# Two heads per softmax step in an attention and expert kernel: 64-row score tiles, and division after the product with v

## The chip, the cores and the metric

The kernel runs on one core of a Trainium2 chip. The metric is the time of one execution on the device in microseconds. Three runs of the kernel before took 1354.6, 1354.81 and 1356.63 us; the median is 1354.81 us.

The core has a matrix engine (TensorE, PE in the profile; its weight loads are shown as PEld), a vector engine (VectorE, DVE), an activation engine (ScalarE, ACT), a general engine (GpSimd, POOL) and a queue that issues transfers (SyncE, SP). Each runs its own instructions in order and they meet at semaphores. The matrix engine writes to PSUM, a small memory of eight banks, from which DVE and ACT read.

## The reference

Attention with a threshold over 8 batches of 8 heads, 576 positions and 64 values per head, and behind it a two-layer network on all 4608 tokens:

```python
scale = 1.0 / np.sqrt(q.shape[-1])
scores = scale * np.matmul(q, k.transpose(0, 1, 3, 2))
thresh = np.max(scores, axis=-1, keepdims=True) - tau
scores = np.where(scores >= thresh, scores, -1000000000.0)
scores = scores - np.max(scores, axis=-1, keepdims=True)
attn = np.exp(scores)
attn = attn / (np.sum(attn, axis=-1, keepdims=True) + 1e-09)
attn_out = np.matmul(attn, v)                      # (8, 8, 576, 64)

x = attn_out.transpose(0, 2, 1, 3).reshape(8 * 576, 512)
h = x @ w_in                                       # 512 -> 2048
g = h * (1.0 / (1.0 + np.exp(-h)))
return g @ w_out                                   # 2048 -> 512
```

## The kernel before

**Precision.** Products run in pieces. q and k are split into a rounded part and the rest (`hi`, `lo`); so are the attention weights, v, x, the weights of the network and its inner values, in 16 bits. A product is the sum of the partial products of the pieces.

**Visits and tiles.** Attention goes through *visits* of two heads, a pair. Batch 0 is visited twice, first for queries 0 to 255 (`low`) and then for the rest (`high`); from batch 1 on there is one visit (`all`) per pair, 28 in all. A visit consists of tiles of 128 queries of one head against all 576 keys. The last 64 queries of both heads share a tile, so a full visit has nine tiles. There are 288 tiles: 16 low, 20 high and 252 in batches 1 to 7. The low tiles work in float32 throughout (`direct`) and are transposed on PE.

**A tile's way.** 
- `scores` (line 406): the 64 rows of q's `hi` stand above the 64 of its `lo` (`qstack`), k's rows stand there twice, so that a matmul over 128 rows gives both partial products. Four matmuls of 288 columns per tile, eight for the shared one. The result lies in a PSUM buffer of two banks; there are two such buffers (`ps_s`).
- `soft1` (416, 419): DVE takes the negated maximum, then the threshold. `soft1b` (426): ACT takes the exponential. `soft2` (435, 439, 443): DVE sets what is under the threshold to zero and sums the rest, then adds 1e-9 and takes the reciprocal. The score buffer is free after line 435.
- `soft2b` (448): ACT multiplies the tile by the reciprocal of its row's sum, in place. `soft3` (457, 459, 462, 465): the weights are rounded to 16 bits (by POOL, for the first tiles by ACT) and POOL subtracts for the rest. `hl` holds both; SP transposes it into `wT` by a transfer (475). The float32 tile `w` has four buffers, `hl` three, `wT` three.

**Before and behind it.** `load_qk` fetches q and k of one head, each twice for the two halves of the rows. `split_k` and `split_q` (309, 310, 318, 320) make the pieces per head. `split_v` (270, 271) rounds v. `av` (490) multiplies the transposed weights with v, the two heads in the two column halves of the array, 28 matmuls per range of queries; `av_post` (508, 509) makes the two pieces of x. The experts work on ranges of queries in units: `h_unit` (524 to 547) and `o_unit` (562 to 573), twelve matmuls each, 16 + 16 units per range, two ranges of 288 queries per batch.

**Once per batch** `vscale` takes a common scale of v: a maximum per partition on DVE, then `partition_all_reduce` on POOL (line 113), then small operations on DVE (from 116 on).

**The order.** The program is written out in slots, one per tile. In each slot stand the steps of a tile, the loads and splits due, and a number of units of the experts at a rate that is set when a range becomes ready (`rate`: units waiting over the slots until the next range that is more than one slot away). A planner then orders the instructions of each engine by priority and by a modelled time; some steps are given a higher priority (`PRI_S` 500 for scores, 50 and 200 for the parts of the softmax). The weights of the network are decoded and split in slots up to 26 (`W_PLAN`).

```python
for h, use, tl, last in ((ha, u, ta, last_a), (ha + 1, use_b, tb + [4] * (4 in ta), last_b)):
    at(use - LOAD, lambda v=v, h=h: load_qk(v, h))
    at(use - 3, lambda h=h: split_k(h))
    at(use - 2, lambda h=h, tl=sorted(tl): split_q(h, tl))
for j, (c0, n) in enumerate(ranges):
    avs.setdefault(last_b + AV_LAG + j, []).append((v, p, c0, n))
```

## Time and profile before

| | |
|---|---|
| median of three runs | 1354.81 us |
| span of the profiled execution | 1360.4 us (5.6 us above the median, which is 0.4%) |
| granted TensorE clock, mean | 0.950 |
| busy: PE, DVE, ACT, POOL | 1183.7, 1002.8, 817.5, 789.9 us |
| read from HBM, written | 66.72 MB, 9.44 MB |
| DMA packets | 363479, most of them under 512 B |
| transfers issued by SP | 304 transposes, 128 + 128 of q and k, 32 of v, 56 of the output |

The profiled execution's own time is its span; nothing around it is shown. An operation's row in the list of groups gives the line, the engine, the operation, what it writes and reads with shape, the count, the busy time, the mean of one in ns, and the idle time of the engine before it with what ended it. Busy time is that in which at least one instruction of the group was at work, so overlapping instructions count once. In the rows by time the first number is the start, the second the duration. In the rows of stretches, each engine's busy time stands with its count of instructions; the clock, the share of the transfer engines and GB/s end the row.

### The profile page before, as it was taken

To read this page: it belongs to the slowest core of one execution; us is meant where nothing else is said; L and a number is where in the kernel's file an instruction comes from. 1 tells how busy PE (TensorE), PEld (TensorE's weight loads), DVE (VectorE), ACT (ScalarE), POOL (GpSimd) and SP (SyncE) were. 2 spreads that over 40 slices of the span, in tenths; PEclk is the share of its full clock that TensorE was granted. 3 is DMA by queue.
4 is the path that set the end of the run, shared out by engine and by line. 5 is a ranking of instruction groups with operands and counts; after the bars stand their busy time and mean duration, and the time that the engine had idled before them with its cause. 6 is when DMAs were issued, how large, how long until landed. Compare 5 with 4: busy or idle time off the path is not lost.

```text
span 1360.4 us, 26858 instructions
## 1 busy us (share of the span) xinstructions
PE 1183.7 (87%) x9392; PEld 899.9 (66%) x9392; DVE 1002.8 (74%) x2619; ACT 817.5 (60%) x1493; POOL 789.9 (58%) x964
## 2 busy tenths in 40 slices
PE   3774787898599979898899969899799999999998
PEld 2453555666477757676677757677577777777777
DVE  4987997897598967968497856869478787872421
ACT  3776775675476756656375745757367666662432
POOL 2647984787478656754476646556467666661000
PEclk9887888999799999999899979999799999999999
DMA  6454955778467656664475556565466565543000
GB/s 226 140 185 125 197 129 94 146 139 170 88 133 155 122 106 129 131 128 86 99 132 124 118 96 136 101 127 121 82 122 116 115 129 115 106 88 53 6 19 18
DMA packets 363479, 158.15 MB, mean 116 GB/s; under 512 B 329552, under 2 KB 338256, under 8 KB 363344
## 3 DMA queue, kind: packets, MB, share of 16 engines
q1 hardware_dynamic: 363344, 156.43, 55.5%
q8 instruction: 74, 1.21, 0.4%
q14 instruction: 61, 0.50, 0.1%
HBM read 66.72 MB, written 9.44 MB: 56 GB/s over the span
## 4 chain that ended last, share of the span: by engine, by line
DVE 35%; PE 34%; issue 13%; ACT 6%; POOL 6%; DMA 5%; SPq 2%; POOLq 0%; ACTq 0%; DVEq 0%
PE o L562 15%; PE h L524 8%; DVE w L435 8%; DVE sm L416 6%; DVE gbuf L547 6%; PE s L406 5%; PE a L490 5%; DVE qstack L310 3%; DVE th L533 3%; DMA vraw<-in_vL 2%; DMA wT<-hl 2%; ACT w L426 2%; POOL hl L459 2%; POOL hl L462 2%; ACT w L448 2%
## 5 line engine op out<-in xcount | busy, mean ns | idle before, releaser
L524 PE MATMUL h<-x,wst 128*128 128x288 f16 (+2 forms) x3072 | 422.3, 290 | 22.6 <-DVE th L533 19.1
L562 PE MATMUL o<-gbuf,wst 128*128 128x288 f16 (+2 forms) x3072 | 419.4, 293 | 22.4 <-DVE gbuf L547 16.1
L562 PEld LDWEIGHTS <-wst 128*128 128x128 f16 x3072 | 296.4, 100 | 117.1 <-issue 27.1
L459 POOL TENSOR_SCALAR hl<-w 128x576 f16<-128x576 f32 x264 | 187.3, 710 | 317.9 <-ACT w L448 69.1
L524 PEld LDWEIGHTS <-wst 128*128 128x128 f16 x3072 | 290.7, 99 | 119.2 <-issue 37.5
L462 POOL TENSOR_TENSOR hl<-w,hl 128x512 f16<-128x512 f32 x272 | 332.0, 1220 | 28.0 <-issue 13.9
L426 ACT ACTIVATE w<-s,sm 128x576 f32<-128x576 f32 x288 | 211.0, 736 | 204.5 <-POOL hl L465 135.4
L435 DVE SCALAR_TENSOR_TENSOR w<-s,sm,w 128x576 f32<-128x576 f32 x288 | 232.6, 810 | 110.4 <-ACT w L426 108.7
L448 ACT ACTIVATE w<-w,sm 128x576 f32<-128x576 f32 x288 | 218.2, 770 | 86.5 <-DVE sm L443 81.6
L416 DVE TENSOR_REDUCE sm<-s 128x1 f32<-128x576 f32 x288 | 215.1, 748 | 44.4 <-PE s L406 42.3
L406 PE MATMUL s<-khi,qstack 128*128 128x288 f32 x608 | 160.4, 346 | 70.0 <-DVE w L435 36.9
L547 DVE SCALAR_TENSOR_TENSOR gbuf<-th,gbuf 128x288 f16<-128x288 f32 (+2 forms) x256 | 167.3, 656 | 20.9 <-ACT gbuf L541 20.2
L406 PEld LDWEIGHTS s<-khi,qstack 128*128 128x128 f32 x608 | 98.5, 198 | 98.8 <-issue 71.4
L490 PE MATMUL a<-wT,v 128*64 128x288 f16 (+1 forms) x1680 | 142.4, 294 | 16.1 <-DMA wT<-hl 15.0
L532 ACT ACTIVATE th<-h,msc 128x288 f32<-128x288 f32 (+2 forms) x256 | 126.3, 495 | 49.5 <-DVE gbuf L547 30.0
L541 ACT ACTIVATE gbuf<-th 128x288 f16<-128x288 f32 (+2 forms) x252 | 109.9, 438 | 44.5 <-DVE th L533 43.9
L406 PE MATMUL s<-klo,qstack 128*128 128x288 f32 x608 | 134.2, 304 | 0.0
L533 DVE SCALAR_TENSOR_TENSOR th<-th,h 128x288 f32<-128x288 f32 (+2 forms) x256 | 113.2, 444 | 27.6 <-ACT th L532 25.4
L490 PEld LDWEIGHTS <-v 128*64 128x64 f16 x1680 | 91.3, 110 | 56.7 <-issue 41.9
L465 POOL TENSOR_TENSOR hl<-w,hl 128x64 f16<-128x64 f32 x272 | 115.3, 424 | 0.0
L406 PEld LDWEIGHTS s<-klo,qstack 128*128 128x128 f32 x608 | 102.2, 197 | 0.0
L320 POOL TENSOR_TENSOR klo<-kraw,khi 128x576 fp32r<-128x576 f32 x64 | 95.6, 1493 | 1.4 <-ACT khi L318 1.3
(82 smaller groups left out, 868.8 us busy)
## 6 DMA issues: line engine op xcount, KB each, us to landing
qraw<-in_qT SPq DMA_DIRECT2D x128, 144.0 KB, 3.0
kraw<-in_kT SPq DMA_DIRECT2D x128, 144.0 KB, 3.0
vraw<-in_vL SPq DMA_DIRECT2D x32, 320.0 KB, 3.5
wraw<-in_w_out SPq DMA_DIRECT2D x16, 512.0 KB, 4.0
out_t<-ot SPq DMA_DIRECT2D x56, 144.0 KB, 2.0
wT<-hl SPq DMA_TRANSPOSE x304, 3.3
gbuf<-in_w_in SPq DMA_DIRECT2D x8, 512.0 KB, 5.1
wraw<-in_w_in SPq DMA_DIRECT2D x8, 512.0 KB, 4.9
```

The lines of the kernel that those rows point to most:

```text
L406: nc.tensor.matmul(s_ps[:, j, :HALF], lhs, kk[:, j * HALF : (j + 1) * HALF], start=(n == 0), stop=(n == len(seq) - 1),)
L416: nc.vector.tensor_reduce(out=negm, in_=s_ps[:, :, :HALF], op=ALU.max, axis=AX.XY, negate=True)
L426: nc.scalar.activation(wtile[t].rearrange("p (j c) -> p j c", j=2), sps[t][:, :, :HALF], AF.Exp, bias=small[t][:, 0:1],)
L435: nc.vector.scalar_tensor_tensor(out=w3, in0=s_ps[:, :, :HALF], scalar=sm[:, 1:2], in1=w3, op0=ALU.is_ge, op1=ALU.mult, accum_out=sm[:, 2:3],)
L448: nc.scalar.activation(w, w, AF.Copy, scale=r)
L459: nc.gpsimd.tensor_scalar(out=fl[:, 0:S], in0=w, scalar1=1.0, scalar2=1.0, op0=ALU.mult, op1=ALU.mult)
L462: nc.gpsimd.tensor_tensor(out=fl[:, 640:1152], in0=w[:, 0:512], in1=fl[:, 0:512], op=ALU.subtract)
L490: nc.tensor.matmul(a_ps[odd * D : (odd + 1) * D, :n], vt[:, lo_v, odd, kv, :], wT[v, b * H + 2 * p + odd][:, kw, c0 - base : c0 - base + n ...
L524: nc.tensor.matmul(ph[:, :n], wi(c, f, lo_w), x16[b, lo_x][:, c, c0 : c0 + n], start=(k == 0), stop=(k == 11),)
L533: nc.vector.scalar_tensor_tensor(out=th[:, :n], in0=th[:, :n], scalar=1.0, in1=ph[:, :n], op0=ALU.add, op1=ALU.mult,)
L547: nc.vector.scalar_tensor_tensor(out=g[:, 1, :n], in0=th[:, :n], scalar=2.0**-14, in1=g[:, 0, :n], op0=ALU.mult, op1=ALU.subtract,)
L562: nc.tensor.matmul(ps[:, :n], wo(f, d, lo_w), g[:, lo_g, :n], start=(f == 0 and k == 0), stop=(f == NF - 1 and k == 2),)
```

## The change

The unit of work of the attention becomes a *step*: the same 128 queries of both heads of a pair. A full visit has four steps of two heads and one of the last 64 queries of both, five in place of nine.

- **q and k.** Both heads' rows are loaded once, one head in rows 0 to 63 and the other in 64 to 127, and split once per pair. q's rounding is with ACT and its rest always with DVE (before, with POOL in batch 0). The last queries are laid out by the host with zeros, so that one 128-row matmul serves both heads.
- **Scores.** Four partial products, each over 64 rows, for each head and half of the keys: 16 matmuls per step, the heads in turn in the upper and lower rows. The PSUM buffer has four banks, and there is one.
- **Softmax.** One reduction over both heads. The threshold goes to POOL. Exponential and select are still one per head. The sums of a visit are kept (`sums`).
- **Division.** The scaling of the weights goes, and with it the reciprocal per tile (the low visits keep both). `invert_sums` inverts the sums of a range, writes them to DRAM, and `load_rows` reads them back as rows spread over the partitions; `av_post` multiplies the product with v by them on DVE, rounds on ACT, and subtracts on POOL.
- **Rounding of the weights** is with ACT, over both heads; the subtraction is one POOL operation. `w` has two buffers of two heads, `hl` two of two heads. In the rows of `hl` the rest follows the rounded part at column 576 and not at 640, so blocks 5 to 8 of v's rounded part are shifted copies that two transfers make in `split_v`.
- **v** is loaded once more for its split from batch 1 on.
- **Ranges** are queries 0 to 255 and 256 to 575 in all batches. The first is handed on after a visit's second step, so the ranges of a batch become ready five slots apart. `wT` has three buffers for each range.
- **Slots.** A step of two heads takes two slots, the shared one takes one; the plan of the weights, rates and gaps stay. Scores of the next step are written after the select of this one.

```diff
+QW = S + 64
-LOAD = 5  # tiles that the loads of q and k run ahead
+LOAD = 6
+ROW_LAG, AV_LAG2 = 2, 4
+RANGES = [(0, 256), (256, 320)]
...
-    ps_s = ctx.enter_context(tc.tile_pool(name="ps_s", bufs=2, space=PSUM))
+    ps_s = ctx.enter_context(tc.tile_pool(name="ps_s", bufs=1, space=PSUM))
...
-        o = sb.tile([P, 2, 2, 5, D], F16, tag="v16", name=f"v16_{b}_{p}", bufs=4)
-        nc.scalar.activation(o[:, 0], t, AF.Copy, scale=s)
+        hi = sb.tile([P, 2, 9, D], F16, tag="vhi", name=f"vhi_{b}_{p}", bufs=2)
+        lo = sb.tile([P, 2, 5, D], F16, tag="vlo", name=f"vlo_{b}_{p}", bufs=2)
+        nc.scalar.activation(hi[:, :, 0:5, :], t, AF.Copy, scale=s)
...
+        nc.sync.dma_start(out=hi[0:D, :, 5:9, :], in_=hi[D:P, :, 0:4, :])
+        nc.sync.dma_start(out=hi[D:P, :, 5:9, :], in_=hi[0:D, :, 1:5, :])
...
-    def load_qk(v, h):
-        for r in range(2):
-            nc.sync.dma_start(out=kr[r * D : (r + 1) * D, :], in_=kT[b, hh])
-            nc.sync.dma_start(out=qr[r * D : (r + 1) * D, :], in_=qT[b, hh])
+    def load_qk(v):
+        kr = sb.tile([P, S], F32, tag="kraw", name=f"kraw_{v}", bufs=1)
+        nc.sync.dma_start(out=kr, in_=kT[b, p])
+        qr = sb.tile([P, QW], F32, tag="qraw", name=f"qraw_{v}", bufs=1)
+        nc.sync.dma_start(out=qr, in_=qT[b, p])
...
+    def split_q(v):
+        c0 = P * VISITS[visits[v][2]][0]
+        src = qkraw[v][0][:, c0:]
+        nc.scalar.activation(qh[:, c0:], src, AF.Copy, scale=gate)
+        nc.vector.scalar_tensor_tensor(
+            out=ql[:, c0:], in0=src, scalar=gate, in1=qh[:, c0:].bitcast(F32),
+            op0=ALU.mult, op1=ALU.subtract,
+        )
...
     def scores(t):
+        v, i = steps[t]
+        s_ps = ps_s.tile([P, 2, 2, 512], F32, tag="s", name=f"s_{t}")
+            seq = [(qh, kh), (qh, kl), (ql, kh), (ql, kl)]
+        w = P if i == 4 else D
+        for n, (qq, kk) in enumerate(seq):
+            for j in range(2):
+                for h in range(heads(t)):
+                    r = slice(h * w, (h + 1) * w)
+                    nc.tensor.matmul(
+                        s_ps[:, h, j, :HALF], qq[r, i * P : (i + 1) * P],
+                        kk[r, j * HALF : (j + 1) * HALF],
+                        start=(n == 0), stop=(n == len(seq) - 1),
+                    )
     def soft1(t):
+        w = sb.tile([P, 2, S], F32, tag="w32", name=f"w32_{t}", bufs=2)
         nc.vector.tensor_reduce(
+            out=sm[:, 0:nh], in_=s_ps[:, :nh, :, :HALF], op=ALU.max, axis=AX.XY, negate=True
+        )
+        nc.gpsimd.tensor_scalar(
+            out=sm[:, 2 : 2 + nh], in0=sm[:, 0:nh], scalar1=-1.0, scalar2=ntau,
+            op0=ALU.mult, op1=ALU.add,
+        )
...
+    def invert_sums(v, a, b):
+        nc.vector.tensor_scalar(
+            out=r[:, a:b], in0=sums[v][:, a:b], scalar1=1e-9, scalar2=None, op0=ALU.add
+        )
+        nc.vector.reciprocal(out=r[:, a:b], in_=r[:, a:b])
+        for h in range(2):
+            if a < 8:
+                nc.sync.dma_start(
+                    out=d[h, 64 * a : 64 * min(b, 8)].rearrange("(i p) -> p i", p=P),
+                    in_=r[:, a + h : min(b, 8) : 2],
+                )
...
+    def load_rows(v, g):
+        R = sb.tile([P, WID], F32, tag="rows", name=f"rows_{v}_{g}", bufs=2)
+        for h in range(2):
+            nc.sync.dma_start(
+                out=R[h * D : (h + 1) * D, :n], in_=d[h, c0 : c0 + n].partition_broadcast(D)
+            )
     def soft2b(t):
+        if steps[t][0] not in direct:
+            return
     def soft3(t):
+        hl = sb.tile([P, 2, 9 * P], F16, tag="hl", name=f"hl_{t}", bufs=2)
+        nc.scalar.activation(hl[:, :nh, 0:S], w[:, :nh], AF.Copy)
+        nc.gpsimd.tensor_tensor(
+            out=hl[:, :nh, S : 2 * S], in0=w[:, :nh], in1=hl[:, :nh, 0:S], op=ALU.subtract
+        )
...
     def av_post(v, p, g, a_ps):
+        x = sb.tile([P, WID], F32, tag="th", name=f"x32_{v}_{c0}", bufs=4)
+        nc.vector.tensor_tensor(
+            out=x[:, :n], in0=a_ps[:, :n], in1=rows.pop((v, g))[:, :n], op=ALU.mult
+        )
+        nc.scalar.activation(hi, x[:, :n], AF.Copy)
+        nc.gpsimd.tensor_tensor(out=lo, in0=x[:, :n], in1=hi, op=ALU.subtract)
...
+            if v not in direct:
+                at(u, lambda v=v, a=a, e=e: invert_sums(v, a, e))
+                at(u + ROW_LAG, lambda v=v, g=g: load_rows(v, g))
+                lag = AV_LAG2
+            avs.setdefault(u + lag, []).append((v, p, g))
             if p == NPAIR - 1:
+                ready.append((u + lag + 1, b, *RANGES[g]))
```

More of the change, by code (lines that the diff above doesn't have):

```diff
@@ L340, in scale_direct @@
+    direct = set()
     def scale_direct(v):
-        for j in range(2):
-            own = direct[v][0][j * D : (j + 1) * D, 256 * j : 256 * (j + 1)]
-            nc.scalar.activation(own, own, AF.Copy, scale=gate[j * D : (j + 1) * D, :])
+        own = qkraw[v][0][:, 0 : RANGES[0][1]]
+        nc.scalar.activation(own, own, AF.Copy, scale=gate)
     def soft3_direct(t):
         w = wtile.pop(t)
-        v, parts = tiles[t]
-        base, n = VISITS[visits[v][2]][2][0]
-        main = bank([P, 4, P], f"tm_{t}")
@@ new lines, in soft3_direct @@
+        n = RANGES[0][1]
+        for h in range(2):
+            main = bank([P, 4, P], f"tm_{t}_{h}")
+            for k in range(4):
+                nc.tensor.transpose(main[:, k, :], w[:, h, k * P : (k + 1) * P], ident)
+            last = bank([P, P], f"tl_{t}_{h}")
+            nc.tensor.transpose(last, w[:, h, S - P : S], ident)
+            if (v, h) not in wT:
+                wT[v, h] = sb.tile([P, 5, n], F32, tag="wThigh", name=f"wTd_{v}_{h}", bufs=3)
+            out = wT[v, h][:, :, i * P : (i + 1) * P]
+            nc.scalar.activation(out[:, 0:4, :], main, AF.Copy)
+            nc.scalar.activation(out[:, 4, :], last, AF.Copy)
@@ L425, in soft1b @@
     def soft1b(t):
[L426 to L429 removed]
+        for h in range(heads(t)):
+            nc.scalar.activation(
+                wtile[t][:, h].rearrange("p (j c) -> p j c", j=2), sps[t][:, h, :, :HALF], AF.Exp,
+                bias=small[t][:, h : h + 1],
+            )
     def soft2(t):
+        v, i = steps[t]
+        nh = heads(t)
         s_ps = sps.pop(t)
@@ new lines, in soft2 @@
+        for h in range(nh):
+            w3 = w[:, h].rearrange("p (j c) -> p j c", j=2)
+            nc.vector.scalar_tensor_tensor(
+                out=w3, in0=s_ps[:, h, :, :HALF], scalar=sm[:, 2 + h : 3 + h], in1=w3,
+                op0=ALU.is_ge, op1=ALU.mult, accum_out=total[:, h : h + 1],
+            )
+        if v not in direct:
+            small.pop(t)
+            return
+        nc.vector.tensor_scalar(
+            out=sm[:, 6:8], in0=total, scalar1=1e-9, scalar2=2.0**-12, op0=ALU.add, op1=ALU.mult
+        )
@@ new lines, in load_rows @@
+    def load_rows(v, g):
+        c0, n = RANGES[g]
+        _, d = rdram[v]
+        R = sb.tile([P, WID], F32, tag="rows", name=f"rows_{v}_{g}", bufs=2)
+        for h in range(2):
+            nc.sync.dma_start(
+                out=R[h * D : (h + 1) * D, :n], in_=d[h, c0 : c0 + n].partition_broadcast(D)
+            )
+        rows[v, g] = R
+    def soft2b(t):
+        if steps[t][0] not in direct:
+            return
+        r = small.pop(t)[:, 8:10]
+        for h in range(2):
+            w = wtile[t][:, h]
+            nc.scalar.activation(w, w, AF.Copy, scale=r[:, h : h + 1])
@@ L593, in attention_moe, with gap @@
     start = {}
+    begin = []
+    u = 0
+    def gap(n):
+        nonlocal u
+        for _ in range(n):
+            steps.append(None)
+            begin.append(u)
+            u += 1
     for v, (b, p, kind) in enumerate(visits):
         if kind == "high" and p == 0:
-            tiles.extend([None] * GAP)
-            first_high = len(tiles)
+            gap(GAP)
+            first_high = u
         if b == 1 and p == 0:
-            tiles.extend([None] * GAP1)
-        ta, tb, ranges = VISITS[kind]
@@ L632, in attention_moe @@
+    NT = u
     for b in range(B):
@@ L690, in live @@
     def live(t):
-        return 0 <= t < NT and tiles[t] is not None
+        return 0 <= t < len(steps) and steps[t] is not None
     scores(0)
-    t = 0
-    while t < NT + 8 or units or ready:
+    k = 0
+    while k < len(steps) or units or ready or avs:
+        t = begin[k] if k < len(steps) else NT + k - len(steps)
+        nxt = begin[k + 1] if k + 1 < len(steps) else max(t + 1, NT)
         while ready and ready[0][0] <= t:
@@ L698, in attention_moe @@
             units.extend(moe_units(b, c0, n))
-            nxt = [r[0] for r in ready if r[0] > t + 1]
-            rate = len(units) / max(1, (nxt[0] if nxt else NT + 8) - t)
+            then = [r[0] for r in ready if r[0] > t + 1]
+            rate = len(units) / max(1, (then[0] if then else NT + 8) - t)
             rate *= RATE
```

349 lines of the change are left out of this document (134 added, 215 removed).

## The prediction

> **What bounds the kernel now.** I read the page's busy times first, then the chain that ended last, then stretches of the span, then single tiles in the timeline.
>
> ```profile
> span 1360.4 us, 26858 instructions
> PE 1183.7 (87%) x9392; PEld 899.9 (66%) x9392; DVE 1002.8 (74%) x2619; ACT 817.5 (60%) x1493; POOL 789.9 (58%) x964
> DVE 35%; PE 34%; issue 13%; ACT 6%; POOL 6%; DMA 5%; SPq 2%; POOLq 0%; ACTq 0%; DVEq 0%
> ```
>
> No engine owns the chain: DVE and PE carry a third each. So the stretches matter. The columns are length, then busy us of PE, PEld, DVE, ACT, POOL.
>
> ```profile
> 0.00:50.00 50.00, 20.44 (x67) 12.84 (x68) 31.80 (x72) 20.58 (x37) 20.34 (x28) 0.83 0.65 208
> 50.00:100.00 50.00, 39.90 (x245) 26.62 (x245) 45.53 (x122) 42.62 (x83) 27.46 (x26) 0.93 0.50 158
> 100.00:150.00 50.00, 29.35 (x177) 20.57 (x173) 41.25 (x90) 32.05 (x57) 37.89 (x38) 0.76 0.59 138
> 150.00:200.00 50.00, 37.72 (x279) 27.30 (x276) 49.87 (x116) 36.48 (x67) 45.22 (x48) 0.86 0.73 166
> 467.50:1083.70 616.20, 557.02 (x4573) 428.82 (x4572) 462.52 (x1248) 374.23 (x684) 370.81 (x467) 0.97 0.59 115
> 1083.70:1215.00 131.30, 129.98 (x1097) 100.94 (x1094) 105.27 (x285) 87.22 (x160) 89.54 (x113) 1.00 0.58 112
> ```
>
> Up to 200 us DVE is the busiest (168.5 us) while PE idles 72.6 us. Batches 3 to 6 (467 to 1084) take 154 us each, 14.8 of them PE idle. Batch 7 takes 131.3 us with 1.3 idle: there PE is the bound. What differs is one thing per batch:
>
> ```profile
> 792.61 0.67 POOL L459 TENSOR_SCALAR hl<-w 128x576 f16<-128x576 f32 x1 [0.60 <-DMA wT<-hl]
> 799.61 0.38 POOL L113 PARTITION_ALL_REDUCE v_all<-v_one  x1 [6.33 <-issue]
> 807.15 1.14 POOL L462 TENSOR_TENSOR hl<-w,hl 128x512 f16<-128x512 f32 x1 [7.17 <-issue]
> 803.06 0.82 PE L406 MATMUL s<-khi,qstack 128*128 128x288 f32 x2 [6.09 <-DVE sm L419]
> 810.35 0.82 PE L406 MATMUL s<-khi,qstack 128*128 128x288 f32 x2 [5.00 <-DVE sm L443]
> ```
>
> Around the reduction over partitions (once per batch, before batch 7's tiles for the last time) POOL does nothing useful for 13.9 us (793.28 to 807.15), and PE stands 11.1 us of it. The change keeps this.
>
> Now the loop through the score buffers. One tile, and the first and the last of the 252 reductions of batches 1 to 7:
>
> ```profile
> 444.22 0.53 PE L406 MATMUL s<-khi,qstack 128*128 128x288 f32 x2
> 444.58 0.42 PE L406 MATMUL s<-klo,qstack 128*128 128x288 f32 x2
> 446.92 0.74 DVE L416 TENSOR_REDUCE sm<-s 128x1 f32<-128x576 f32 x1
> 447.78 0.74 ACT L426 ACTIVATE w<-s,sm 128x576 f32<-128x576 f32 x1 [1.62 <-DVE sm L416]
> 448.56 0.82 DVE L435 SCALAR_TENSOR_TENSOR w<-s,sm,w 128x576 f32<-128x576 f32 x1 [0.27 <-ACT w L426]
> 450.53 0.52 PE L406 MATMUL s<-khi,qstack 128*128 128x288 f32 x2
> ...
> 197.25 0.73 DVE L416 TENSOR_REDUCE sm<-s 128x1 f32<-128x576 f32 x1
> ...
> 1214.69 0.75 DVE L416 TENSOR_REDUCE sm<-s 128x1 f32<-128x576 f32 x1
> ```
>
> The pitch is (1214.69-197.25)/251 = 4.05 us; with two buffers in turn, one buffer's cycle is 8.1 us. Bare work in a cycle is 0.78 scores + 0.75 + 0.74 + 0.89 (select and its accumulator read) = 3.16 us, so 4.9 us of a mean cycle are waits in queues, swap included. The tile shown has a cycle of 6.31 us (444.22 to 450.53), so 3.15 of waits.
>
> **The change, part by part.** Durations (line, engine, shapes, count | busy, mean ns):
>
> ```profile
> L416 DVE TENSOR_REDUCE sm<-s 128x1 f32<-128x576 f32 x288 | 215.1, 748 | 44.4 <-PE s L406 42.3 <-PE s L394 1.0
> L435 DVE SCALAR_TENSOR_TENSOR w<-s,sm,w 128x576 f32<-128x576 f32 x288 | 232.6, 810 | 110.4 <-ACT w L426 108.7
> L435 DVE DVE_READ_ACCUMULATOR w<-s,sm,w 128x1 f32 x288 | 23.3, 81 | 0.0
> L419 DVE TENSOR_SCALAR sm<-sm,ntau 128x1 f32<-128x1 f32 x288 | 59.0, 207 | 2.8
> L443 DVE RECIPROCAL sm<-sm 128x1 f32<-128x1 f32 x288 | 44.2, 156 | 2.5
> L439 DVE TENSOR_SCALAR sm<-sm 128x1 f32<-128x1 f32 x288 | 41.4, 145 | 1.2
> L310 DVE SCALAR_TENSOR_TENSOR qstack<-qraw,gate,qstack 64x576 fp32r<-64x576 f32 x56 | 68.8, 1228 | 5.8 <-ACT qstack L309 3.9 <-DMA wT<-hl 0.3
> L448 ACT ACTIVATE w<-w,sm 128x576 f32<-128x576 f32 x288 | 218.2, 770 | 86.5 <-DVE sm L443 81.6 <-DVE v_sc L131 4.3
> L457 ACT ACTIVATE hl<-w 128x576 f16<-128x576 f32 x8 | 5.4, 674 | 0.0
> L459 POOL TENSOR_SCALAR hl<-w 128x576 f16<-128x576 f32 x264 | 187.3, 710 | 317.9 <-ACT w L448 69.1 <-issue 67.5 <-DMA wT<-hl 58.7
> L462 POOL TENSOR_TENSOR hl<-w,hl 128x512 f16<-128x512 f32 x272 | 332.0, 1220 | 28.0 <-issue 13.9
> L465 POOL TENSOR_TENSOR hl<-w,hl 128x64 f16<-128x64 f32 x272 | 115.3, 424 | 0.0
> L490 PE MATMUL a<-wT,v 128*64 128x288 f16 x1568 | 130.6, 293 | 12.9 <-DMA wT<-hl 12.9
> L490 PEld LDWEIGHTS <-v 128*64 128x64 f16 x1680 | 91.3, 110 | 56.7 <-issue 41.9 <-DMA wT<-hl 6.7 <-DMA kraw<-in_kT 0.9
> 716.51 0.52 PE L406 MATMUL s<-khi,qstack 128*128 128x288 f32 x2
> 717.39 0.43 PE L406 MATMUL s<-klo,qstack 128*128 128x288 f32 x2
> ```
>
> *DVE, per visit of nine tiles.* Before: 9 x (748+207+810+81+145+156) = 19.3 us, plus two q splits, 2.5. After: four double steps with one reduction of 1152 (estimate 1.35 us: twice 748 less one fixed part of some 0.15, the length of L439) and two selects with their reads (1.78), one single step (1.64), one q split on 640 columns (1.36 by L310's rate), two short pairs of add and reciprocal (0.6): 16.1. It saves 5.7 us per visit.
>
> *ACT.* The nine scalings (6.9) go; rounding comes in their place: four of 1152 (estimate 1.15 each, 674 plus the rate) and one of 576, 5.3 us. About -1.6, and half the q and k splits.
>
> *POOL.* Nine times 0.71+1.22+0.42 = 21.2 us become four subtractions of 1152 (1.22 x 2.25 = 2.75) and one of half, 12.4, with two of the product (about 0.7 each). The threshold moves here from DVE, five short ones; it follows the reduction and is wanted by the select, so it hides beside the 0.74 us exponential, unless it queues behind a 2.75 us subtraction of the step before: between 0 and 2.0 us, taken as 0.4 inside the waits below.
>
> *PE.* Sixteen 64-row matmuls replace eight of 128 rows. If the two row halves run side by side, a step costs what the eight-matmul tile costs now, 1.31 us (716.51 to 717.82), against twice 0.78 (444.22 to 445.00). Most of the 0.25 us between them is the tail that overlaps what follows; I take 0.1 us, 120 times, 12 us. The nearest row for side by side is the product with v in column halves: 1680 loads of 110 ns would be 185 us in a line and are busy 91.3. The other end is no overlap at all, eight more slots of 0.13 us (two matmuls of 0.29 in 0.42 us, the row of 444.58) in 120 steps, +125 us. I take the first, since L490 is the nearest. The Trainium skill, in TensorEngine Tiling (Array Packing), Key Properties, says that tiles load weights and multiply in parallel, with which L490 agrees, and that a change of tiling mode drains the engine; that speaks against this change and is a rival below.
>
> *DMA and SP.* 192 loads of q and k go, and half their bytes; v is loaded twice from batch 1 on; the sums make a trip through DRAM (about ten small transfers per visit) and v's shifted blocks two more. SP waits in order: behind a read that waits for its write stand the transposes. Two buffers of the rounded weights and two to four slots of lead cover it; taken as nothing, and if that cover fails ACT's rounding stops for one landing, a few us per visit at most.
>
> *The score buffer.* Two buffers of one tile become one of two. Bare cycle of a double step: 1.32 + 1.35 + 0.74 (second exponential beside the first select) + 1.78 = 5.2 us; single: 1.32+0.75+0.74+0.89 = 3.7. With waits w per step a visit takes 4 x 5.2 + 3.7 + 5w = 24.5 + 5w.
>
> *Waits.* In batch 7 DVE is busy 2.92 us of each 3.65 us tile; of a cycle of two, 3.7 of 7.3 us (0.50) is work of others than the tile. Afterwards others are 9.6 us per visit (462.5/16 = 28.9 in batches 3 to 6, less the tiles' 19.3), or up to 4 us more, since the tiles' means overlap in the busy time: at most 13.6, in five steps 2.7 of about 7.5 us each, 0.36. Waits that go with the share fall to 0.72, those that go with share/(1-share) to 0.56. From the 3.15 us of the undisturbed tile: w = 2.27 or 1.76; I take 2.0. The bounds are 0 and 4.9.
>
> *Sum by the loop.* Start of batch 1: 197 less the DVE work saved in the DVE-bound beginning (16 low tiles 34.4 to 27.5, 20 high tiles 42.9 to 31.6, new q splits and inversions +5.7) = 185. Then 28 x 24.5 = 686, 140w, six swaps at 13.9 = 83. After the last reduction: some 14 us to the last product and its output, then one group of experts, 320 wide:
>
> ```profile
> 1333.10 23.53 PE o L562 x192
> ```
>
> 2 x 23.53 x 320/288 = 52 (the first layer has as many matmuls). Sum 1020 + 140w: 1300 at w = 2.0, 1266 to 1338 at the two scalings.
>
> *Sum by PE.* 1183.7 - 12 busy, idle 60 in the beginning (72.6 less the 12 saved), 11 x 5 at swaps, 10 elsewhere: 1297. The two limits meet, and where they meet each adds to the other; between 1300 and 1338 I take 1320. The runs' median is 1354.8, 5.6 under this span, so 1315 in their terms.
>
> **The rivals.**
> 1. *One buffer couples PE to the softmax (slower).* Now scores of a tile wait for the select before last; then for the one just made. Each us of w costs 140 us; from w = 2.43 on it is slower than the 1360.4 of now. With the waits of the shown tile unchanged (3.15) the span is 1461; at 2.8, 1412. For it: the loop already waits longer than it works. Besides, experts of the first range come ready five slots before the second, so that 30 of a batch's 64 units are queued in the first two visits' beginning, ahead of products whose buffers the next visit needs. Against: DVE and POOL lose a fifth of their attention work.
> 2. *Row halves don't overlap, or the change of mode drains.* No overlap: 1297 + 125 = 1422. A drain by a matmul's length (L490's 293 ns) twice in 152 steps is 89 us: 1386. The first would contradict the only two-tile row there is. For the drain the Trainium skill's sentence speaks; no row here has row tiles.
> 3. *More is gained.* If w falls to 1 and the swaps overlap with queued experts, PE alone is the bound: 1297 less 40, 1257.
> 4. *Nothing comes of it.* PE had 1.3 us idle in batch 7; if the swap alone makes the rest, and the beginning stays with the weights' decoding, 1350 to 1365 remains.
>
> **Numbers.** Forecast (1285 to 1345 in the runs' terms) 0.44; more gained 0.08; nothing 0.12, a third of it faster and half within 0.2% (about what a measurement of this kernel tells from none); rival 1 0.28; rival 2 0.08. Faster 0.44+0.08+0.04 = 0.56, same 0.06, slower 0.38. The range leaves out 0.08 below 1285, and above 1410 about a third of rival 1 and part of rival 2.
>
> **What would show it.** Right: the 1152 reduction near 1.35 us; 64-row matmuls in pairs a few ns apart, a step's scores 1.3 us; double steps of batch 2 to 6 at about 7 to 7.5 us outside swaps; the last expert group alone after the last product. Wrong: PE idle before scores released by the select in every step; the select waiting on POOL's threshold; transposes held at SP behind reads of the sums; two scores matmuls 0.13 us apart.

## The result, and the profile after

The changed kernel takes 1830.32 us (median of four runs, 1823.79 to 1832.6) against 1355.72 us of the kernel before in the same comparison: a ratio of 1.346, 95% interval 1.342 to 1.351. It is a third slower, far beyond the forecast's 1315 us and its range to 1410 us.

The first lines of the page of the changed kernel (span; then each engine's busy time, share and instructions):

```profile
span 1821.7 us, 27213 instructions
PE 1286.9 (71%) x10352; PEld 954.7 (52%) x10352; DVE 944.5 (52%) x1736; ACT 742.3 (41%) x1289; POOL 554.3 (30%) x486
```

DVE, ACT and POOL have less to do than before (1002.8, 817.5 and 789.9 us), as the change means them to. PE has 103 us more, and every engine's share is lower. Of the 461 us by which the span grew, 358 are idle time of PE (534.8 us in place of 176.7), so most of the added time is waiting.

The span falls into three stretches: up to the first reduction of batch 1, the 28 visits of batches 1 to 7, and what comes from their last reduction on. Columns: stretch, length, then busy us (and instructions) of PE, PEld, DVE, ACT, POOL, the granted clock of TensorE, the share of the DMA engines, GB/s. The kernel before:

```profile
0.00:203.65 203.65, 130.75 (x786) 89.46 (x786) 172.06 (x404) 135.06 (x247) 134.48 (x141) 0.85 0.62 167
203.65:1219.15 1015.50, 915.43 (x7453) 702.09 (x7452) 788.03 (x2124) 634.36 (x1143) 648.67 (x815) 0.96 0.61 119
1219.15:1360.40 141.25, 137.47 (x1158) 108.32 (x1155) 42.73 (x96) 48.11 (x104) 6.71 (x9) 1.00 0.11 23
```

The changed kernel:

```profile
0.00:257.37 257.37, 147.53 (x1023) 105.30 (x1024) 176.70 (x323) 127.09 (x221) 116.22 (x118) 0.82 0.53 142
257.37:1716.39 1459.02, 1041.85 (x8560) 775.44 (x8561) 735.99 (x1344) 580.02 (x993) 432.95 (x364) 0.85 0.51 86
1716.39:1821.70 105.31, 97.52 (x769) 73.95 (x768) 31.83 (x70) 35.15 (x76) 5.17 (x5) 0.98 0.11 22
```

The visits take 1459 us in place of 1015.5, and in them PE idles 417 us in place of 100. What PE waits for, in the changed kernel and then in the one before (us in total, times, longest):

```profile
PE a L506 <- DMA wT<-hl: 255.0, 48, 15.1
...
PE s L371 <- DVE w L413: 107.3, 45, 9.0
```

```profile
PE s L406 <- DVE w L435: 36.9, 26, 10.6
...
PE a L490 <- DMA wT<-hl: 15.0, 5, 8.8
```

Two things grew: the product with v waits for the transposed weights, and the scores wait for the select that frees the one score buffer. The first is the larger. Its other side is SP's queue in the changed kernel, where the reads of the sums (line 455) stand still until their writes have landed:

```profile
SPq L455 <- DMA rs<-rsum: 402.4, 97, 9.6
```

One such place in SP's timeline (start, us), and the same moment in stretches of 2 us:

```profile
1015.69 0.58 SPq L440 DMA_DIRECT2D rs<-rsum  x1
1016.32 0.49 SPq L445 DMA_DIRECT2D rs<-rsum  x1
1019.91 6.20 SPq L455 DMA_DIRECT2D rows<-rs  x2
1026.16 2.80 SPq L491 DMA_TRANSPOSE wT<-hl  x2
```

```profile
1016.00:1018.00 2.00, 2.00 (x16) 1.30 (x14) 0.83 (x3) 1.83 (x4) 0.00 (x0) 0.97 0.38 52
1018.00:1020.00 2.00, 0.21 (x2) 0.00 (x0) 1.93 (x5) 1.70 (x3) 0.00 (x0) 1.00 0.00 0
...
1024.00:1026.00 2.00, 2.00 (x23) 1.61 (x23) 1.42 (x3) 0.47 (x1) 0.00 (x0) 1.00 0.00 0
```

From the last write to the transposes 9.8 us go by (1016.32 to 1026.16), and from 1018 on the DMA engines move little in them (shares of 0.14 and less): SP is not behind a full pipe. The first reading, which run 11 corrects, was that it waits for a slow small transfer.

### The profile page after: what moved, and what is told of

Same layout as the page of the kernel before. It is cut to its first block, busy times and chain, and to the rows that moved or that the text cites. A ratio compares the mean times of both kernels' runs of the same rounds, so it can differ in the third digit from the quotient of the medians.

```text
span 1821.7 us, 27213 instructions
## 1 busy us (share of the span) xinstructions
PE 1286.9 (71%) x10352; PEld 954.7 (52%) x10352; DVE 944.5 (52%) x1736; ACT 742.3 (41%) x1289; POOL 554.3 (30%) x486
## 5 line engine op out<-in xcount | busy, mean ns | idle before, releaser
L476 POOL TENSOR_TENSOR hl<-w,hl 128x1152 f16<-128x1152 f32 (+1 forms) x152 | 326.1, 2146 | 520.6 <-ACT hl L475 452.2
L549 PE MATMUL h<-x,wst 128*128 128x320 f16 (+1 forms) x3072 | 438.4, 301 | 55.8 <-DVE th L558 25.5
L587 PE MATMUL o<-gbuf,wst 128*128 128x320 f16 (+1 forms) x3072 | 412.6, 294 | 4.9 <-DVE gbuf L572 4.8
L506 PE MATMUL a<-wT,vhi 128*64 128x320 f16 (+1 forms) x1080 | 131.7, 365 | 288.2 <-DMA wT<-hl 255.0
L383 DVE TENSOR_REDUCE sm<-s 128x2 f32<-128x1152 f32 (+1 forms) x160 | 197.1, 1232 | 240.9 <-PE s L371 240.7
L475 ACT ACTIVATE hl<-w 128x1152 f16<-128x1152 f32 (+1 forms) x152 | 161.4, 1062 | 221.2 <-DVE w L413 205.5
L572 DVE SCALAR_TENSOR_TENSOR gbuf<-th,gbuf 128x256 f16<-128x256 f32 (+1 forms) x256 | 205.3, 819 | 42.4 <-ACT gbuf L566 40.8
L557 ACT ACTIVATE th<-h,msc 128x256 f32<-128x256 f32 (+1 forms) x256 | 122.6, 499 | 73.6 <-PE h L549 66.7
L566 ACT ACTIVATE gbuf<-th 128x320 f16<-128x320 f32 (+1 forms) x252 | 105.2, 437 | 106.6 <-DVE th L558 106.0
L558 DVE SCALAR_TENSOR_TENSOR th<-th,h 128x256 f32<-128x256 f32 (+1 forms) x256 | 110.7, 447 | 72.5 <-ACT th L557 67.0
```

Source lines behind the costliest of these rows:

```text
L383: nc.vector.tensor_reduce(out=sm[:, 0:nh], in_=s_ps[:, :nh, :, :HALF], op=ALU.max, axis=AX.XY, negate=True)
L475: nc.scalar.activation(hl[:, :nh, 0:S], w[:, :nh], AF.Copy)
L476: nc.gpsimd.tensor_tensor(out=hl[:, :nh, S : 2 * S], in0=w[:, :nh], in1=hl[:, :nh, 0:S], op=ALU.subtract)
L506: nc.tensor.matmul(a_ps[odd * D : (odd + 1) * D, :n], vt[:, odd, kw, :], wT[v, odd, g][:, kw, :], start=(k == 0), stop=(k == len(seq) - 1),)
L549: nc.tensor.matmul(ph[:, :n], wi(c, f, lo_w), x16[b, lo_x][:, c, c0 : c0 + n], start=(k == 0), stop=(k == 11),)
L557: nc.scalar.activation(th[:, :n], ph[:, :n], AF.Tanh, scale=moe_sc[b][:, 0:1])
```

## The experiments

The theory after the first profile (A): SP's wait for the sums' writes holds the transposes back. The rival (B): the one score buffer couples PE to the softmax, and the trip hides in that. The first four runs do one part alone. In each run the kernel before ran beside on the same chip; it took 1361 to 1368 us there (medians).

**1. The trip left out.** The product is scaled by constant rows, so the division is missing from the result.

```diff
-        nc.sync.dma_start(out=d[h, ...], in_=r[:, ...])          # invert_sums
-        nc.sync.dma_start(out=R[...], in_=d[h, ...].partition_broadcast(D))
+        rows[v, g] = rone                                        # load_rows
```

> The changed kernel without the trip of the sums through DRAM: the product with v is multiplied by a constant in place of the row sums' inverses, so the division by the sums is left out; all else stays. Theory A (SP's queue: the reads of the sums wait there for their writes, 402 us in all, the transposes stand behind, and PE stands at the products with v): SP's waits of 402 us are gone, PE's wait for the transposes falls from 255 us to under 80, the span falls by 250 to 450 us, to 1370-1570. Theory B (the single score buffer sets the pace): PE's wait for the select stays, the span stays above 1700. If both act, the time ends between, 1570-1700.

Measured: 1567.45 us, ratio 1.151 (1.142 to 1.159). Its stretches and waits:

```profile
0.00:249.03 249.03, 149.92 (x1023) 106.45 (x1023) 173.95 (x316) 126.73 (x221) 117.06 (x118) 0.80 0.53 145
249.03:1461.54 1212.51, 989.63 (x8560) 749.59 (x8561) 728.98 (x1235) 576.34 (x993) 433.67 (x364) 0.91 0.48 96
1461.54:1565.80 104.26, 97.84 (x769) 73.90 (x768) 31.63 (x68) 35.12 (x76) 5.17 (x5) 0.98 0.08 21
```

```profile
PE s L371 <- DVE w L413: 119.1, 55, 9.8
PE a L484 <- DMA wT<-hl: 82.7, 37, 7.9
```

The trip is worth 256 us of span (1821.7 - 1565.8), 246.5 of them in the 28 visits. The wait for the select is as long as with the trip. So the loss has two parts: 256 us by the trip, 205 by the rest (1565.8 - 1360.4).

**2. The trip alone**, added to the kernel before (same writes, a read of 64 columns, its result unused).

```diff
+        at(u + 4, lambda v=v: invert_sums(v, 0, 4))
+        at(u + 6, lambda v=v: load_rows(v, 0))
+        at(last_b + 1, lambda v=v: invert_sums(v, 4, 9))
+        at(last_b + 3, lambda v=v: load_rows(v, 1))
```

> The kernel before with the same trip added: per full visit, six small writes of inverted sums (of one tile, repeated) to DRAM and four reads back of 64 columns each, which nothing uses. Theory A: SP waits some 300-400 us for the writes, the transposes behind them come late, the span rises by 100-400 us, to 1460-1760. Theory B: the trip is off every path, 1350-1400.

Measured: 1714.96 us, ratio 1.259 (1.250 to 1.268), some 350 us. SP's wait for the writes is there again:

```profile
SPq L477 <- DMA rs<-rsum: 301.5, 75, 9.6
```

The trip costs no less in a kernel with two score buffers; it needs nothing else of the change.

**3. One score buffer alone**, in the kernel before.

```diff
-    ps_s = ctx.enter_context(tc.tile_pool(name="ps_s", bufs=2, space=PSUM))
+    ps_s = ctx.enter_context(tc.tile_pool(name="ps_s", bufs=1, space=PSUM))
```

> The kernel before with one score buffer of one tile in place of two. Bare work of a tile's cycle is 3.2 us; with the waits of 2.4 to 4.9 us a tile would take 5.6 to 8 us in place of 4.05. Theory B: the span rises by 300-900 us, PE waiting for the select. Theory A says nothing against it for one tile; if the span rises by less than 100 us, the number of score buffers can't be a large part of the change's loss either.

Measured: 1697.53 us, ratio 1.246 (1.236 to 1.256). PE's wait for the select goes from the 36.9 us above to this:

```profile
PE s L406 <- DVE w L435: 228.3, 78, 7.1
```

So a second buffer is worth some 333 us to tiles of one head. How much of that a buffer of two heads gives back, no run separates.

**4. Division in the rounding.** A way without DRAM that gives the full result: ACT rounds with the reciprocal as its scale, POOL scales `w` before it subtracts.

```diff
-        nc.scalar.activation(hl[:, :nh, 0:S], w[:, :nh], AF.Copy)
+            nc.scalar.activation(hl[:, h, 0:S], w[:, h], AF.Copy, scale=r)
+            nc.gpsimd.tensor_scalar(out=w[:, h], in0=w[:, h], scalar1=r, scalar2=1.0, ...)
```

> The changed kernel with the division put back ahead of the product, inside the rounding: a reciprocal per step on DVE, ACT's rounding takes it as its scale (one instruction per head, 0.67 us each, in place of one of 1.16), POOL multiplies in place (0.7 us per head) before its subtraction. No trip. Theory A: as without the trip, 1370-1570, POOL some 200 us busier. Theory B: above 1700.

Measured: 1577.11 us, ratio 1.158 (1.149 to 1.167). With the extra work of ACT and POOL it is 10 us over leaving the division out, and still 253 us under the changed kernel with its trip.

**5. Weights per head**, on the kernel of 4: `w` becomes a tile for each head, so that the first select need not wait for the second exponential on its account. POOL's subtraction is then one per head too.

> The kernel with the scale in the rounding (1576 us), with the float32 weights of the two heads in a tile each. In the runs so far the first select starts 0.74 us after the end of the first head's exponential, which is the length of the second's: both write one tile, and the select waits for both. If that wait belongs to the loop through the score buffer, 0.74 us go from each of 120 double steps: -89 us, to 1470-1510. If the loop isn't what sets the pace, or the slack goes into another wait of the loop, less than -30 us.

Measured: 1564.81 us, 12 less, far from the 89 hoped for. Two exponentials and the first select of a double step in its timeline:

```profile
955.21 1.37 ACT L397 ACTIVATE w<-s,sm 128x576 f32<-128x576 f32 x2 [0.85 <-DVE sm L385]
...
956.69 0.82 DVE L410 SCALAR_TENSOR_TENSOR w<-s,sm,w 128x576 f32<-128x576 f32 x1 [1.24 <-ACT w L397]
```

The select still starts after both have ended (955.21 + 1.37 = 956.58), and so it does in all 128 double steps of this run. Something else that the two share makes it wait.

**6. Two score buffers of one head, heads in turn**, on the kernel of 5. The side-by-side order of the matmuls goes.

```diff
+        s_ps = [ps_s.tile([P, 2, 512], F32, tag="s", ...) for h in range(heads(t))]   # bufs=2
+        for h in range(heads(t)):
             for n, (qq, kk) in enumerate(seq):
                 for j in range(2):
-                    for h in range(heads(t)):
```

> As the kernel with weights per head, and the score buffer cut into two of one head (two banks each): the heads' scores go one after the other and no longer side by side in the row halves, so PE has 120 x 1.04 = 125 us more, and reduction and threshold are per head. Theory B (one buffer makes the loop pay all its waits in series): with two heads in flight PE's wait for the select falls, and the span falls by 50-150 us in spite of PE's 125 us. If the single buffer isn't the cause, the span rises by 60-130 us.

Measured: 1494.86 us, 70 less than 5, although PE works 118 us more (1351.6 against 1233.1). PE is now busy for 90% of the span.

**7. The maximum on PE.** In the kernel before, POOL's reduction over partitions becomes a transpose on PE, a maximum on DVE and a matmul with ones.

```diff
-            nc.gpsimd.partition_all_reduce(allp, one, P, bass.bass_isa.ReduceOp.max)
+            nc.tensor.transpose(mp[0:1, 0:P], one, ident)
+            nc.vector.tensor_reduce(out=top, in_=mp[0:1, 0:P], op=ALU.max, axis=AX.X)
+            nc.tensor.matmul(mp[:, 256:257], onesf, top, start=True, stop=True)
...
+            nc.vector.tensor_copy(allp, mp[:, 256:257])
```

> The kernel before, the maximum over the partitions of v taken with a transposition and a product on PE and not with POOL's reduction, after which POOL stands 13.9 us per batch. If the difference of batches 3 to 6 to batch 7 (154 to 131 us each) is that standstill, the span falls by 80-140 us, to 1220-1280; if PE's queue merely fills other gaps, by less than 30.

Measured: 1289.13 us, ratio 0.947 (0.945 to 0.949), 72 us less where 80 to 140 were expected. This kernel beats both. The new operations in the view of their tile (ns: shortest, median, longest; the matmuls with ones come twice each):

```profile
L116 PE MATMUL v_mp<-v_top,onesf x16: 245/266/369, 29.9 to 1028.9; 1*128 1x1 f32 x16
...
L113 PE MATMUL v_mp<-ident,v_one x8: 271/273/273, 22.8 to 1025.1; 128*1 128x128 f32 x8
L115 DVE TENSOR_REDUCE v_top<-v_mp x8: 259/269/275, 27.3 to 1028.4; 1x1 f32<-1x128 f32 x8
```

**8. The reads from POOL's queue** in place of SP's, in the changed kernel, so that the transposes do not stand behind them.

> The changed kernel with the reads of the sums issued by POOL in place of SP; the writes stay with SP. Theory A with the order as cause: SP's wait for the writes goes, the transposes come on time, the span falls to 1560-1620 as without the trip. If the landing itself is too late for the product's output, or POOL now stands before its subtractions and the threshold, it stays above 1700.

Measured: 1948.72 us. The wait moved with the reads, and now POOL's threshold stands behind it:

```profile
POOL rows L455 <- DMA rs<-rsum: 509.1, 77, 13.2
...
DVE w L413 <- POOL sm L386: 390.0, 73, 11.0
```

**9. The trip with two score buffers**: the edit of 6 on the changed kernel.

> The changed kernel, its trip kept, with two score buffers of one head in place of one of two, the heads' scores one after the other (PE +125 us). Without the trip this cut gained 70 us (1565 to 1495). If the two causes add, 1824 falls by about 70, to 1730-1780. If two heads in flight cover the late transposes, it falls by more than 150. If the trip alone sets the pace, it stays within 30 us.

Measured: 1840.2 us, no gain. Without the trip the same edit (there on weights per head) gained 70. So while the trip is there it sets the pace, and the gains do not add.

**10. The threshold back on DVE**, on the kernel of 1 (division left out).

> The kernel without the trip (division left out, 1567 us) with the threshold back on DVE. The select waited for POOL's threshold 42.6 us in all, 20 times. If that lies in the loop, the span falls by 20-45 us; if the second head's exponential ends last in most steps anyway, less than 15; 0.2 us of DVE per step in the loop could also cost up to 30.

Measured: 1545.43 us, 22 less.

**11. The rows read one visit late.** In the changed kernel, a visit reads the sums of the visit before, whose writes have long landed (so it divides by other sums).

```diff
-        _, d = rdram[v]
+        _, d = rdram[v - 1 if old else v]
```

> The changed kernel with all transfers of the trip in number and size, but each read takes the sums of the visit before (from the second full visit on), whose writes have landed long ago: the division uses the wrong visit's sums, with a factor of 1/1024 on their inverses. Theory A in the form 'the wait of SP's queue for the landing': SP's 402 us of waits fall under 60 and the span falls to 1560-1620, as without any trip. If the transfers themselves or their issue cost (some 300 small ones more), it stays above 1700.

Measured: 1842.3 us. SP's wait went and PE's stayed:

```profile
SPq L456 <- DMA rs<-rsum: 68.2, 24, 6.5
...
PE a L507 <- DMA wT<-hl: 255.1, 45, 11.9
```

Theory A falls in this form: 334 us of SP's waiting can go without a gain. SP's queue now stands in the issue of single transposes, as here:

```profile
995.85 10.60 SPq L492 DMA_TRANSPOSE wT<-hl  x1
```

So it is the transfers themselves that hold back the rest. Open was which of them.

**12. The maximum on PE**, on the kernel of 1.

> The kernel without the trip (division left out, 1567 us) with the maximum over the partitions on PE. It gained 72 us in the kernel before. If the swap's standstill is paid by the loop as much here, it falls by 60-110 us, to 1455-1505; the rest over 1362 is then the loop through the single score buffer.

Measured: 1492.87 us, 75 less, as in the kernel before (72).

**13 to 15. Writes only; reads only; writes in runs.** In 13 the sums are written and never read (constant rows). In 14 the rows are read from a tile written once at the start. In 15 the whole trip stays, but a write is one transfer of 128 runs of 16 or 20 bytes (the rows come back in another order). The result of all three lacks the right division. The edit shown is that of 15.

```diff
-                    out=d[h, 64 * a : 64 * min(b, 8)].rearrange("(i p) -> p i", p=P),
-                    in_=r[:, a + h : min(b, 8) : 2],
+            out=d[P * a : P * b].rearrange("(p c) -> p c", p=P), in_=r[:, a:b]
```

> The changed kernel with the sums' inverses still written to DRAM every visit (16-64 transfers of 4-byte elements), but never read back: the products are scaled by constant rows, so the division is left out of the result. If the scattered 4-byte writes hold the DMA queues: 1760 to 1840 us, the wait of PE's products for the transposes near 250 us as in the changed kernel. If it is the reads behind them (a read that must see its write landed, or 64-fold broadcast): 1565 to 1610, near the 1567 of the kernel without the trip, transposes' wait under 100 us. In between: both have a part.

> The mirror image: the rows are read from DRAM at the same places, four reads a visit, but from a tile that is written once at the start; the per-visit writes are left out (so the division is by a constant). If the reads by themselves hold the queues: 1760 to 1840. If they cost only behind scattered writes: 1565 to 1610.

> The trip whole, with the same bytes, the same waits of read for write and the same places on SP, but each write is one transfer of 128 runs of 16 or 20 bytes in place of two or three of 4-byte elements (the rows come back in another order, so the division is by wrong sums). If the number of 4-byte elements is the cost: 1570 to 1650. If it is the trip to DRAM and back as such (landing latency, SP's wait in order): 1780 to 1840.

Measured: 1831.52, 1566.16 and 1588.04 us. The writes alone cost all that the trip costs, the reads nothing (14 keeps DVE's inversion as well), and writes in runs 22 us over the reads alone. SP's wait for the landing of the writes, 402.4 us in the changed kernel, is 55.9 us in 15. PE's waits for the transposes, of the writes alone and then of the writes in runs:

```profile
PE a L501 <- DMA wT<-hl: 242.5, 43, 12.9
```

```profile
PE a L500 <- DMA wT<-hl: 110.9, 45, 7.3
```

And how long SP needs to issue one transpose of a double step (shortest, median, longest), again 13 and then 15:

```profile
L486 SPq DMA_TRANSPOSE wT<-hl x240: 1242/1334/9932, 141.5 to 1720.0; - x120
```

```profile
L485 SPq DMA_TRANSPOSE wT<-hl x240: 1243/1338/2762, 142.4 to 1495.7; - x120
```

The median is the same; behind element writes single issues take up to 9.9 us. The pages count the packets: 403681 in 13, 365919 in the kernel of 1, 37762 more, of which the elements are 34816 (28 visits of 1152 and 4 of 640) and sixteen for each of the 184 writes another 2944. They cost 261 us of span (1827.2 - 1565.8), 7.5 ns an element.

By the packets' own times that is not their own work. In the trace of 13 a four-byte packet takes 9 ns in the median, and all of them together 32 us of an engine's time (mean of the 16 DMA engines; 9 us in run 1). The 256-byte packets, as many in both runs, go from 464 to 641 us, single ones up to 6.6 us in place of 2.1. In the changed kernel they take 484 us; there SP stands in waits for the landings.

The Trainium skill, in DMA: Bandwidth & Descriptors, Specifications, puts the least transfer for full rate at 512 bytes, with a read-modify-write below. The trace agrees that small writes to DRAM are dear, but that threshold does not separate the cases: runs of 16 and 20 bytes are far below 512 too, and 15 pays a twelfth. Run 15 differs from 13 in more than the size of a packet: it has 60 writes in place of 184, 8496 packets over the reads alone in place of 37762, and words that are neighbours in DRAM come from one partition. Which of these carries the cost was not tried. In the same page, the Trainium skill says under Issuing engines are not separate DMA queues that issuing from several engines saves only issue time. Run 8 (1948.72 us) gained nothing by it, but it is no test of that: POOL's own wait was in its way, and the writes stayed with SP.

**16. A score tile for each head**, one buffer of two heads, on the kernel of 5 (division in the rounding).

```diff
-        s_ps = ps_s.tile([P, 2, 2, 512], F32, tag="s", name=f"s_{t}")
+        s_ps = [ps_s.tile([P, 2, 512], F32, tag=f"s{h}", ...) for h in range(heads(t))]
```

> The kernel with weights per head (1565 us, no trip), with the score buffer cut into one tile for each head, still one buffer of two heads and row halves side by side. If the first select waited for the second exponential because both read one score tile: 4 x 28 x 0.74 = 83 us less, up to 18 given back for two reductions of 576 in place of one of 1152 (120 x 0.15): 1480 to 1510. If the wait has another cause: 1560 to 1585.

Measured: 1498.22 us, 67 less. One step in its timeline:

```profile
949.18 0.53 PE L371 MATMUL s<-khi,qhi 64*128 64x288 f32 x2
...
951.08 0.52 PE L371 MATMUL s<-khi,qhi 64*128 64x288 f32 x2
...
953.11 0.81 DVE L411 SCALAR_TENSOR_TENSOR w<-s,sm,w 128x576 f32<-128x576 f32 x1
...
953.52 0.73 ACT L398 ACTIVATE w<-s,sm 128x576 f32<-128x576 f32 x1
```

Here the first head's select runs before the other head's exponential. The select starts behind the second exponential in 4 of 128 double steps, where it was all 128 in run 5. So it was the shared score tile (both exponentials read it, and the select waits for its readers) that kept the first select back.

The gain is not that wait alone. The matmuls now go head by head (two of a kind at 949.18, the other head's two at 951.08, where the kernels before show four together), although the program writes them in turn; it seems that the order of each head's follows its own tile. With that the kernel is nearly the one of 6 (two tiles of one head each), and so are its time (1498.22 and 1494.86 us) and PE's work (1344.6 and 1351.6 us). The 67 us are what the freed select and the heads running apart gain together, less some 112 us more of PE's work.

**17. The kernel of 16 with the maximum on PE.**

> The kernel with a score tile per head (1498 us, no trip, division in the rounding) with the maximum over the partitions on TensorE in place of POOL's reduction. The reduction was worth 72 to 75 us in the kernel before and in the one without the trip. If its stop of PE is worth the same where PE is busy 90% of the span: 1420 to 1435, still over the kernel before. If PE's own work (1345 us busy of 1497) leaves less to gain: 1440 to 1480. Under 1355 would say that the change in this form beats the kernel before.

Measured: 1416.98 us, ratio 1.037 (1.025 to 1.050), 81 less than 16 and 3 below the range expected. This gives the full result, and PE is its bound:

```profile
PE 1327.1 (94%) x10376; PEld 1012.7 (72%) x10376; DVE 942.3 (67%) x2065; ACT 780.5 (55%) x1409; POOL 786.4 (56%) x938
```

With the trip, the shared score tile and POOL's reduction taken out, heads in pairs are still 3.7% over the kernel before, and some 10% over the kernel of 7, which has the same maximum (1416.98 over 1289.13). The threshold, worth 22 us in run 10, stays on POOL here. PE works 1327 us here and 1167 there, 160 more, 118 of them by run 6 from the heads going in turn; DVE is spared 72 us for it (942.3 against 1014.7) and POOL 8. Side by side with a tile per head was not tried.

## Why the prediction was wrong, step by step

The sum by the loop had three terms, and the three stretches measure them (us):

| term | predicted | no trip (run 1) | changed kernel |
|---|---|---|---|
| to batch 1 | 185 | 249.0 | 257.4 |
| 28 visits | 28 x 24.5 + 140 x 2.0 + 83 = 1049 | 1212.5 | 1459.0 |
| after the last reduction | 66 | 104.3 | 105.3 |
| span | 1300 | 1565.8 | 1821.7 |

**The failing step: DMA and SP.** "Two buffers of the rounded weights and two to four slots of lead cover it; taken as nothing", with "a few us per visit at most" if the cover fails. It cost 246.5 us in the 28 visits, 8.8 each, and 256 in all. The working looked at who waits behind the read. The cost was in the write, four bytes to a packet; the one wait that points at it, SP's 402.4 us, can go without a gain (run 11). The change was read as "about ten small transfers per visit"; counted in packets it is 1152 elements a visit. (Of q's and k's loads 184 went, 256 to 72, and not 192; nothing hung on that.) The profile of before has no such write, so this step had no row for its bound and should have had a wide one.

**The second: waits and the score buffer.** Rival 1 had the right sign and mechanism, with a chance of 0.28, but priced 1461 at most: it moved w alone, and kept the bare cycle, the beginning and the end of the forecast. Run 1 spends 1212.5 us on 28 visits, 163 more than the forecast. One double step of run 1, from its scores to the next:

```profile
960.68 0.53 PE L371 MATMUL s<-khi,qhi 64*128 64x288 f32 x4 [0.54 <-DVE w L413]
...
961.54 0.46 PE L371 MATMUL s<-klo,qlo 64*128 64x288 f32 x4
...
963.49 1.34 DVE L383 TENSOR_REDUCE sm<-s 128x2 f32<-128x1152 f32 x1
...
964.93 1.37 ACT L395 ACTIVATE w<-s,sm 128x576 f32<-128x576 f32 x2 [0.94 <-DVE sm L383]
...
966.41 0.82 DVE L413 SCALAR_TENSOR_TENSOR w<-s,sm,w 128x576 f32<-128x576 f32 x1 [1.25 <-ACT w L395]
...
967.89 0.08 DVE L413 DVE_READ_ACCUMULATOR w<-s,sm,w 128x1 f32 x1
...
969.04 0.53 PE L371 MATMUL s<-khi,qhi 64*128 64x288 f32 x4
```

The cycle is 8.36 us: 1.32 scores, 1.49 until the reduction starts, 1.34 reduction, 0.10, both exponentials 1.37, 0.11, selects 1.56, 1.07 until the next scores. The prediction's bare 5.2 us had 0.74 for "second exponential beside the first select". They are not side by side: both exponentials come first, 0.63 us more in each of 112 double steps, 71 us, with the shared score tile as the reason (run 16). Its selects are 0.22 us shorter than the 1.78 taken, so a double step's bare work is 5.6 us (1.32 + 1.34 + 1.37 + 1.56), and a visit's 26.1 (4 x 5.6 + 3.7) in place of 24.5. What is left for w: 1212.5/28 = 43.3 us per visit, less 2.7 for the reduction's stop (75 us over 28) and 26.1, is 14.5, so w = 2.9 in five steps against the 2.0 taken. Both scalings by the share of others' work, which gave 2.27 and 1.76, took too much off the 3.15 of the tile shown. The threshold, "taken as 0.4 inside the waits below", was worth 22 us in run 10, under 0.2 a step, so it was not what was short. Run 3 shows how much weight this step deserved.

**The beginning** was short by 64 us even without the trip. The prediction subtracted DVE work saved from a stretch where DVE was the busiest. In run 1 DVE is busy only 174 of those 249 us, so it was not the bound any more. What is, no run took apart. Some 6 of the 64 us are a reading: at 197.25 starts the last reduction of batch 0, and batch 1's first follows at 203.65 (the last of batch 7 at 1219.15, not 1214.69; the pitch is 4.05 us either way).

**The end** was short by 38 us: one range's experts were taken as left. In run 1, PE's groups after the last reduction count 357 and 384 matmuls of the two layers, not 192 and 192; the first range, handed on five slots earlier, was mostly still queued.

**The sum by PE** took 125 us of idle (60, 55 and 10); run 1 idles 328 (1565.8 - 1237.4). It took 12 us off PE's work (1171.7); run 1 has 1237.4, 54 more than before, and the changed kernel 1286.9. Some 35 of the 54 are the change of mode below; the rest was not taken apart.

**What was right.** Groups of the changed kernel by form (count | busy, mean ns):

```profile
L476 POOL TENSOR_TENSOR hl<-w,hl 128x1152 f16<-128x1152 f32 x120 | 285.1, 2376 | 480.1 <-ACT hl L475 411.6 <-issue 60.2 <-DMA wT<-hl 8.2
...
L383 DVE TENSOR_REDUCE sm<-s 128x2 f32<-128x1152 f32 x128 | 173.0, 1352 | 194.1 <-PE s L371 193.9
...
L475 ACT ACTIVATE hl<-w 128x1152 f16<-128x1152 f32 x120 | 139.6, 1163 | 167.9 <-DVE w L413 163.3 <-issue 3.0 <-DMA wT<-hl 1.5
...
L301 DVE SCALAR_TENSOR_TENSOR qlo<-qraw,gate,qhi 128x640 fp32r<-128x640 f32 x28 | 32.0, 1143 | 0.0
```

2.75 us was predicted for the first, 1.35 for the second, 1.15 for the third, 1.36 for the last. The second and third are within 2%, the other two came out 14 and 16% cheaper, and it did not matter.

**Rival 2.** Its first half (row halves not side by side) is refuted: sixteen matmuls take 1.32 us, against 1.31 forecast. The Trainium skill's TensorEngine Tiling (Array Packing), Key Properties, that tiles multiply in parallel, agrees with it. Its second half, a cost of the change of mode, is there, at less than half the price. The experts' weight loads in run 1, behind a 128-row tile and behind a 64-row step:

```profile
954.72 5.14 PEld L527 LDWEIGHTS <-wst 128*128 128x128 f16 x36
961.93 3.83 PEld L527 LDWEIGHTS <-wst 128*128 128x128 f16 x36 [0.17 <-issue]
```

From the start of the last expert matmul before the scores to the start of the first one behind them, run 1 takes 1.17 to 1.19 us around a 128-row tile and 1.46 to 1.48 around a 64-row step (medians of the faster half, in which little else is waited for). That is 0.29 us more a step, although eight single matmuls there and eight pairs here take the same 1.3 us by themselves: some 35 us of PE's time in 120 double steps, by this estimate, where the rival took 0.293 us twice in 152 steps, 89 us. The Trainium skill's sentence in the same section, that a change of tiling mode drains the engine, agrees with this. What it costs the span, no run shows; in run 1 PE has idle time to spare, in run 17 it has little. The prediction found no row with row tiles, but the profile of before has such changes around the product with v in column halves: from the last expert matmul to its first 0.216 us go by, and 0.218 back, where two expert matmuls are 0.122 apart.

**What is confirmed.** The reduction on POOL, "The change keeps this" at 13.9 us a batch, 83 in the sum, is borne out by runs 7, 12 and 17 (72, 75 and 81 us).

## What to carry to other kernels

Count a transfer in packets, not in issues: here, writing columns element by element to DRAM cost 7.5 ns per element, hardly any of it in the packets' own time, and the wait that named the writes was not where the time went. A test that removes the waiting (run 11) and one that removes the transfer (runs 1, 13, 14) are two tests; here only the second found the cause. And sparing an engine work gained nothing here, where the loop through a single buffer, not the engine, was the limit; first ask what stands in the cycle of that buffer, every reader of the shared tile included.

## What the runs showed of the hardware

- Writes of four bytes cost the other transfers more than themselves: they took 32 us of packet time in run 13, while the issue of a double step's transpose took up to 9.9 us beside them and 2.8 us beside runs of 16 to 20 bytes, with equal medians. What inside the DMA engines holds, the trace does not show.
- Going from 128-row matmuls to 64-row ones and back cost PE 0.29 us a step in run 1.
- The granted clock fell with the stops: 0.965 in run 7, 0.95 before, 0.90 in run 1, 0.85 after. Which follows from which was not tried.
- The cost of a part depends on what else is bound: two buffers gained 70 us without the trip and nothing with it, and the trip cost 256 us in the changed kernel and 350 in the one before.
